# A list scheduler that fixes a kernel's instruction order: refitted costs, result time and hand-over apart, and a charge for changes of kind on TensorE

## The chip, the cores and the metric

The kernel runs on one core of one Trainium2 chip. A core has TensorE (PE, matrix products; its weight loads appear as PEld), VectorE (DVE), ScalarE (ACT), GpSimd (POOL) and SyncE (SP), each with an instruction queue of its own, and 16 DMA engines. The metric is the device time of one execution in microseconds, lower is better. Of several executions the median counts.

## The reference

Attention with a capped score over 4 batches of 12 heads (48 heads), 448 positions, head size 64, followed by a feed-forward layer with layer norm on the 1,792 tokens of 768 features, with 3,072 hidden features:

```
scores = scale * q @ k.T                      # per batch and head, 448 x 448
scores = cap * tanh(scores / cap)
attn = exp(scores - max); attn /= attn.sum(-1) + 1e-9
x = (attn @ v), heads side by side            # 1792 x 768
xn = (x - mean) / sqrt(var + 1e-6) * g_ln
out = x + relu(xn @ w_ch1) @ w_ch2            # all fp32
```

## The kernel before, in words

**Precision.** The feed-forward products have fp32 accuracy out of a narrower matmul type: every operand is split into a rounded part (hi) and a remainder (lo), and a product is three matmuls, hi*hi, hi*lo and lo*hi, that add up in one PSUM bank. Rounding and remainder of an operand are two instructions of ScalarE or VectorE (L488 and L495). The scores and the product with v run on plain fp32 operands; from head 28 on the scores too are split.

**Attention.** The 48 heads run in 12 groups of four. For each group TensorE makes blocks of scores (`qk`, L723 and, split, L749; "rest" blocks for the last 64 rows), ScalarE takes tanh (L768) and exp (L776) of them, TensorE multiplies by v (`pv`, L552 and L559), adds up the denominators (`sums`, L636, L640) and transposes for the division (`turn`, L662, L676). L609 copies a group's result out of its PSUM bank.

**Feed-forward, first six token tiles (of 128 tokens).** `up` (L1019 to L1021, six matmuls of 128x384 per operation) and `down` (L1048 to L1050) run between the attention groups, from the first norm (its transposes are L899) at about 76 us to about 500 us.

**Feed-forward, last eight token tiles.** In the last stage, from about 505 us, the product runs as a seven-product scheme of Strassen's kind, block by block over 12 blocks of hidden features. Per block there are two sorts of operation on TensorE:
- *W product n* (n = 1 to 7; `product` in `stage`, L1237, L1238, L1240): nine matmuls of 128x512 that make hidden features. Products 1, 6, 7 and 4 add up one after another in one PSUM bank (`pa`), 5 and 3 in a second, 2 has a third. After each of the four the copy `aside` (ScalarE, L1254) reads `pa`, and it must have done so before the next product adds to it. VectorE's `plus` (L1258) and `join` (L1274) combine the copies, `operand` splits the combination (L488, L495), and `hidden` (L1030, L1032) does ReLU and split.
- *T product k of tile m* (`product` in `thin`, L1330 to L1332): three matmuls of 128x384 that multiply a split operand by the second weight. A T product that starts a bank is evacuated by a copy (ScalarE, L1338) or a sum (VectorE, L1342) into one half of a staging buffer `st`; there are six of these. When both halves are in, GpSimd's `store` (L1347) adds the buffer to the output in DRAM by DMA, and the buffer is free once that has landed.

**What sets the order.** The program is written as a list of operations (`add`), each with an engine, a cost in ns, the buffers that it reads, writes and takes, and a due time worked out from the table `PLAN`. The class `Order` then plays the list through before the kernel is built: at each moment every free engine takes, of its ready operations, the one with the earliest due time whose buffers can be had. A consumer becomes ready at the producer's end plus `SAME` on the same engine (130 ns on VectorE, 155 on ScalarE, 0 on TensorE) or `CROSS` (210 ns) from another engine. A PSUM bank or staging buffer comes back when its last user's end, plus `CROSS`, has passed. `lag` is added to an operation's end: 170 ns for the W and T products (`PLAN["lag"]`), 2,500 ns for a store. The costs are straight lines in the operand's width n (`VEC1`, `VEC2`, `VECC` for VectorE, `ACTS`, `ACTP`, `ACTC` for ScalarE, `POOL1` for GpSimd, `MM` and `F4` for TensorE). The sequence in which this play takes the operations is then the program's order on each engine and each DMA queue. Nothing of the play runs on the chip: there each engine executes its fixed list and waits on semaphores.

The two lines that carry the timing of the play:

```python
free[e] = o.end = t + cost
c.ready = max(c.ready, o.end + (SAME[e] if e == c.engine and not o.dma else CROSS))
```

Of the kernel before, what the change touches and what calls it, by code (L numbers as in the profile page):

```python
# [15 lines left out]
ALU = mybir.AluOpType  # L16
PSUM = bass.MemoryType.PSUM

B, H, S, D = 4, 12, 448, 64
# [5 lines left out]
CC, FC = DM // 128, DFF // 128  # L25
NT = B * S // 128
HG = 4
HALF = DM // 2
# [12 lines left out]
TOK = 512  # L41
# [13 lines left out]
VEC1 = lambda n: 60 + 0.75 * n  # L55
VEC2 = lambda n: 50 + 1.1 * n
ACTS = lambda n: 20 + 0.99 * n
ACTP = lambda n: 20 + 1.0 * n
VECC = lambda n: 95 + 1.17 * n
ACTC = lambda n: 160 + 0.87 * n  # L60
POOL1 = lambda n: 100 + 1.1 * n
POOL2 = lambda n: 148 + 2.104 * n
MM = lambda n: n * 0.4515
F4 = lambda n: n * 1.76
TANH, EXP = 1000, 1260
SAME = {"V": 130, "A": 155, "G": 100, "T": 0, "S": 0}
CROSS = 210
# [28 lines left out]
    ks=3000, again=12000, down=16000, thin=20000, w3=14000, fetch=16000, near=20000, part=20000, w3b=0, both=32000, half=15000, u=2000, t=0, lag=170, landing=2500, chunk=18000, blocks=-42000,  # L96
# [47 lines left out]
class Op:  # L144
    __slots__ = ("engine", "cost", "fn", "due", "bufs", "left", "outs", "ready", "end", "dma", "seq", "wait", "after", "lag")


class Order:
# [9 lines left out]
    def add(self, engines, fn, reads=(), writes=(), allocs=(), due=0.0, dma=0, after=(), lag=0.0):  # L158
        op = Op()
        (op.engine, op.cost), = engines.items()  # L160
        op.fn, op.due, op.dma, op.lag, op.seq = fn, due, dma, lag, len(self.ops)
# [45 lines left out]
    def emit(self, realize, run):  # L207
# [8 lines left out]
        cold, busy, window = False, 0.0, -3000.0  # L216
# [21 lines left out]
        while pending:  # L238
            done = False
            for e in free:  # L240
# [15 lines left out]
                if e == "T":  # L256
# [3 lines left out]
                    cost *= 1 + cold  # L260
                    busy += cost
                free[e] = o.end = t + cost
# [16 lines left out]
                for c in o.outs:  # L279

                    if "P" not in (e, c.engine):
                        c.ready = max(c.ready, o.end + (SAME[e] if e == c.engine and not o.dma else CROSS))
# [97 lines left out]
class Program:  # L380
# [117 lines left out]
    def quad(self, i, at):  # L498
# [92 lines left out]
        else:  # L591
            for p in range(2):
                for blocks in [[j] for j in range(NK)] if i + p == 0 and not self.general else [range(NK)]:
                    add({"T": 200 + len(blocks) * F4(S)}, lambda e, p=p, blocks=blocks: pv(p, blocks),
                        reads=[*v_all, *(done(p) if len(blocks) > 1 else [(es[p], "e", j) for j in blocks])], writes=[pos[p]],
                        allocs=pos, due=dues[p] - PLAN["pv"] - rush)
            add({"T": 100 + F4(S)}, lambda e: pv_rest(), reads=[*v_all, er], writes=pos, due=dues[2] - PLAN["pv"] - rush)
# [31 lines left out]
    def sums(self, parts, rests, due, cost=0, first=None, reads=(), writes=()):  # L629
# [13 lines left out]
        self.last_pv = self.add({"T": 200 + (1 + len(rests)) * F4(S) + cost}, sums, reads=[*parts, *rests, *reads],  # L643
# [3 lines left out]
    def finish(self, i, pairs, ps, due, late):  # L647
# [16 lines left out]
        add({"T": 440}, turn, reads=[(ss, 0), (ss, 2)], writes=[pr], due=due)  # L664
# [6 lines left out]
        for j, tl, p in self.token_tiles(b):  # L671
# [6 lines left out]
            add({"T": len(pairs) * 110}, turn, reads=[(o, x) for o in pairs for x in (0, 2)] + [r] * self.general, writes=[pf], due=due)  # L678
# [899 lines left out]
```

## Time and profile before

| | before |
|---|---|
| device time, median of 3 runs | 857.84 us (857.4 to 928.27) |
| the profiled execution, its own time | 857.77 us |
| its span in the trace | 856.0 us |
| TensorE matmuls busy | 845.8 us (99%), 4700 instructions |
| VectorE busy | 701.7 us (82%) |
| ScalarE busy | 511.9 us (60%) |
| GpSimd busy | 152.1 us (18%) |
| DMA | 148.96 MB, mean 174 GB/s |

The span is the time from the first to the last recorded instruction; 1.8 us of the execution lie around it. Busy time of TensorE counts matmuls, whose ends are modelled; weight loads run beside them. A group of instructions is written as line, engine, operation, output<-inputs, shapes, count; then busy time and mean duration, and behind the bar the idle time of that engine just before these instructions, with what ended most of it. In a timeline a row holds start and duration in us and the same description, with `[idle before <- releaser]` at its end where there was idle time. `two` is a pair of PSUM banks, `y` a combination buffer of the last stage, `hop` a split operand, `w` a split weight, `X` a split combination of xn, `d` a pair of q and k rows, `b` an attention result, and `x` on the way to `out_dram` a staging buffer.

### The profile page before, as it was taken

The numbers are of one execution on the slowest core, as the hardware profiler recorded it, in microseconds if no ns is written. First come the engines' busy times: TensorE is split into PE (matmuls) and PEld (weight loads), VectorE is DVE, ScalarE is ACT, GpSimd is POOL, SyncE is SP. The second block draws the span as 40 slices with busy tenths as digits, with TensorE's granted clock in tenths as the row PEclk, the third lists the DMA queues.
The fourth block names the chain that finished last, engine by engine and source line by source line (L and its number), as shares of the span: only waits on it lengthen the run. The fifth ranks groups of instructions, "written<-read, shape, count | busy, mean of one in ns | idle before, by whom it ended". The sixth has DMA issues, their size and how long they took to land.

```text
span 856.0 us, 12856 instructions
## 1 busy us (share of the span) xinstructions
PE 845.8 (99%) x4700; PEld 706.4 (83%) x4700; DVE 701.7 (82%) x1157; ACT 511.9 (60%) x795; POOL 152.1 (18%) x198
## 2 busy tenths in 40 slices
PE   8999999999999999999999999999999999999997
PEld 5344477979879799799799989998988998999897
DVE  2689798878789878787689878888888888788896
ACT  6887877644654647354436646756575666566550
POOL 0134231111112111111110001223113212312210
PEclk9999999999999999999999999999999999999999
DMA  9597766665675774654562344798878888787984
GB/s 230 138 251 212 197 179 176 186 204 161 184 221 167 221 210 168 184 169 128 179 254 102 102 143 83 164 180 156 169 159 155 165 169 159 139 191 157 181 220 152
DMA packets 55579, 148.96 MB, mean 174 GB/s; under 512 B 7378, under 2 KB 20178, under 8 KB 55506
## 3 DMA queue, kind: packets, MB, share of 16 engines
q1 hardware_dynamic: 41328, 113.43, 44.8%
q0 software_dynamic: 12096, 33.04, 22.8%
q10 hardware_dynamic: 2082, 1.58, 0.6%
q8 instruction: 39, 0.64, 0.3%
q14 instruction: 34, 0.28, 0.1%
HBM read 87.46 MB, written 60.56 MB: 173 GB/s over the span
## 4 chain that ended last, share of the span: by engine, by line
PE 95%; ACT 2%; DVE 1%; issue 0%; POOL 0%; DVEq 0%; ACTq 0%
PE two L1237 7%; PE two L1330 7%; PE two L1240 7%; PE two L1332 7%; PE two L1331 7%; PE two L1238 7%; PE two L1019 6%; PE two L1048 6%; PE two L1050 6%; PE two L1049 6%; PE two L552 6%; PE two L1021 6%; PE two L1020 6%; PE two L723 6%; PE two L676 1%; PE two L636 1%
## 5 line engine op out<-in xcount | busy, mean ns | idle before, releaser
L1347 POOL DMA_DIRECT2D out_dram<-x x84 | 73.4, 998 | 314.6 <-ACT x L1338 227.2
L1338 ACT ACTIVATE x<-two 128x384 f32<-128x384 f32 x168 | 79.6, 487 | 35.6 <-PE two L1332 27.0
L1237 PE MATMUL two<-X,q 128*128 128x512 f32 x252 | 98.9, 392 | 1.2 <-ACT y L1254 1.2
L1019 PE MATMUL two<-hA,q 128*128 128x384 f32 x288 | 99.8, 347 | 0.0
L1240 PE MATMUL two<-X,q 128*128 128x512 f32 x252 | 98.8, 392 | 0.0
L1238 PE MATMUL two<-X,q 128*128 128x512 f32 x252 | 98.6, 391 | 0.0
L1342 DVE TENSOR_TENSOR x<-two,x 128x384 f32<-128x384 f32 x144 | 76.9, 552 | 26.3 <-PE two L1332 22.7
L1048 PE MATMUL two<-w,hh 128*128 128x384 f32 x288 | 98.3, 341 | 0.0
L1050 PE MATMUL two<-w,hl 128*128 128x384 f32 x288 | 97.2, 337 | 0.0
L1049 PE MATMUL two<-w,hh 128*128 128x384 f32 x288 | 97.1, 337 | 0.0
L1021 PE MATMUL two<-hA,q 128*128 128x384 f32 x288 | 96.9, 337 | 0.0
L1020 PE MATMUL two<-lA,q 128*128 128x384 f32 x288 | 96.8, 336 | 0.0
L951 POOL TENSOR_SCALAR raw<-raw 128x768 f32<-128x768 f32 x48 | 49.5, 1031 | 227.9 <-ACT c L947 213.6
L1330 PE MATMUL two<-w,hop 128*128 128x384 f32 x264 | 89.1, 338 | 0.0
L1332 PE MATMUL two<-w,hop 128*128 128x384 f32 x264 | 88.9, 337 | 0.0
L1331 PE MATMUL two<-w,hop 128*128 128x384 f32 x264 | 88.9, 337 | 0.0
L768 ACT ACTIVATE e<-two,sc 128x448 f32<-128x448 f32 (+1 forms) x108 | 75.0, 758 | 20.1 <-PE two L723 20.1
L1053 DVE TENSOR_TENSOR x<-two,x 128x384 f32<-128x384 f32 x144 | 76.2, 548 | 12.4 <-PE two L1050 12.1
L488 ACT ACTIVATE w<-c 128x768 fp32r<-128x768 f32 x38 | 32.1, 845 | 60.3 <-DVE c L956 22.9
L1019 PEld LDWEIGHTS two<-hA,q 128*128 128x128 f32 x288 | 54.1, 188 | 10.9 <-issue 7.1
L776 ACT ACTIVATE e<-e,capt 128x1344 f32<-128x1344 f32 (+1 forms) x35 | 61.1, 1770 | 0.3
L552 PE MATMUL two<-e,v 128*64 128x448 f32 x288 | 59.2, 547 | 1.1 <-ACT e L776 0.8
(179 smaller groups left out, 1852.1 us busy)
## 6 DMA issues: line engine op xcount, KB each, us to landing
raw<-in_w_dram SPq DMA_DIRECT2D x48, 768.0 KB, 5.0
out_dram<-x POOLq DMA_DIRECT2D x84, 384.0 KB, 7.2
kept<-c SPq DMA_DIRECT2D x47, 384.0 KB, 5.5
d<-in_kq_dram SPq DMA_DIRECT2D x48, 224.0 KB, 5.7
d<-kept SPq DMA_DIRECT2D x23, 384.0 KB, 3.2
c<-kept SPq DMA_DIRECT2D x23, 384.0 KB, 7.4
v<-in_v_dram SPq DMA_DIRECT2D x24, 227.5 KB, 5.8
x<-out_dram SPq DMA_DIRECT2D x13, 384.0 KB, 5.1
```

The costliest lines, as they stand in the source:

```text
L1019: nc.tensor.matmul(ps.ap[:, :n], lhsT=w1h.ap[:, wc], rhs=xh.ap[:, c], start=(c == 0), stop=False)
L1020: nc.tensor.matmul(ps.ap[:, :n], lhsT=w1h.ap[:, wc], rhs=xl.ap[:, c], start=False, stop=False)
L1021: nc.tensor.matmul(ps.ap[:, :n], lhsT=w1l.ap[:, wc], rhs=xh.ap[:, c], start=False, stop=(c == CC - 1))
L1048: nc.tensor.matmul(o, lhsT=h[0].ap[:, mc], rhs=w[0].ap[:, hc], start=(f == 0), stop=False)
L1049: nc.tensor.matmul(o, lhsT=h[0].ap[:, mc], rhs=w[1].ap[:, hc], start=False, stop=False)
L1050: nc.tensor.matmul(o, lhsT=h[1].ap[:, mc], rhs=w[0].ap[:, hc], start=False, stop=(f == last))
L1237: nc.tensor.matmul(ps.ap, lhsT=wh.ap[:, wc], rhs=xs[c].ap[:, 0], start=start and c == 0, **o)
L1238: nc.tensor.matmul(ps.ap, lhsT=wh.ap[:, wc], rhs=xs[c].ap[:, 1], start=False, **o)
L1240: nc.tensor.matmul(ps.ap, lhsT=wl.ap[:, wc], rhs=xs[c].ap[:, 0], start=False, **o)
L1330: nc.tensor.matmul(o, lhsT=hh.ap[:, mc], rhs=wh.ap, start=begin, stop=False, **skip)
L1331: nc.tensor.matmul(o, lhsT=hh.ap[:, mc], rhs=wl.ap, start=False, stop=False, **skip)
L1332: nc.tensor.matmul(o, lhsT=hl.ap[:, mc], rhs=wh.ap, start=False, stop=True, **skip)
```

## The change

Five things, all in the numbers by which `Order` plays the list through:

1. The cost lines are other straight lines: `VEC1`, `VEC2`, `ACTS`, `ACTP`, `ACTC`, `POOL1`, `F4`, the tanh and exp, and several single costs; `VECC` goes, and its users take `VEC2`. At a width of 512 a VectorE operation that reads PSUM or two operands was charged 694 ns and is now charged 595; at 384 it was 544 and is 459.
2. A producer's result comes `TAIL` after its engine is free again: 83 ns on VectorE, 110 on ScalarE, 70 on GpSimd, 163 on TensorE. The engine itself goes on to its next operation without the tail.
3. The hand-over to any consumer is `CROSS`, 35 ns instead of 210, on top of the tail; `SAME` goes. From one TensorE operation to the next there is neither.
4. Every TensorE operation has a `kind`. When the kind differs from that of the operation before, `SHIFT` of the kind that is left is charged. Constants of 100 and 200 ns that stood in the costs of single operations go.
5. `PLAN["lag"]` is 0 instead of 170, the GpSimd power of the norm costs 1,600 instead of 800, and the store on GpSimd 860 instead of 1,200.

The core of the diff:

```diff
-VEC1 = lambda n: 60 + 0.75 * n
-VEC2 = lambda n: 50 + 1.1 * n
-ACTS = lambda n: 20 + 0.99 * n
-ACTP = lambda n: 20 + 1.0 * n
-VECC = lambda n: 95 + 1.17 * n
-ACTC = lambda n: 160 + 0.87 * n
-POOL1 = lambda n: 100 + 1.1 * n
+VEC1 = lambda n: 45 + 0.63 * n
+VEC2 = lambda n: 50 + 1.065 * n
+ACTS = lambda n: 92 + 0.835 * n
+ACTP = lambda n: 130 + 0.66 * n
+ACTC = lambda n: 11 + 0.94 * n
+POOL1 = lambda n: 100 + 1.04 * n
-F4 = lambda n: n * 1.76
-TANH, EXP = 1000, 1260
-SAME = {"V": 130, "A": 155, "G": 100, "T": 0, "S": 0}
-CROSS = 210
+F4 = lambda n: n * 1.6786
+TANH, EXP = 888, {1: 1305, 2: 2441}
+TAIL = {"V": 83, "A": 110, "G": 70, "T": 163, "S": 0, "P": 0}
+CROSS = 35
+SHIFT = dict(up=98, down=50, fp=200, split=190, pv=150, rest=160, sums=137, turn=-80)
...
-                    cost *= 1 + cold
+                    cost = cost * (1 + cold) + (SHIFT.get(kind, 0) if o.kind != kind else 0)
+                    kind = o.kind
                     busy += cost
-                free[e] = o.end = t + cost
+                free[e] = t + cost
+                o.end = free[e] + TAIL[e]
...
-                        c.ready = max(c.ready, o.end + (SAME[e] if e == c.engine and not o.dma else CROSS))
+                        c.ready = max(c.ready, o.end + CROSS - (TAIL[e] + CROSS) * (e == c.engine == "T"))
...
-                    add({"T": 200 + len(blocks) * F4(S)}, lambda e, p=p, blocks=blocks: pv(p, blocks),
+                    add({"T": len(blocks) * F4(S)}, lambda e, p=p, blocks=blocks: pv(p, blocks), kind="pv",
...
-            add({"V": VECC(TOK)}, lambda e: nc.vector.tensor_tensor(out=y.ap, in0=ps.ap, in1=y.ap, op=ALU.add),
+            add({"V": VEC2(TOK)}, lambda e: nc.vector.tensor_tensor(out=y.ap, in0=ps.ap, in1=y.ap, op=ALU.add),
```

No instruction is added or removed on any engine; each source line has as many instructions on each engine as it had. What moves is the order. Three places on TensorE follow. Lines of the changed kernel are 2 higher; the numbers in the names are those of the two builds and tell buffers apart within one build.

First, the fourth group of heads, where the trace of before stands at 53 to 60 us. `L723` is a score block, `L662` the transposes of a finished group, `L559` the rest of the product with v, `L636` and `L640` the denominators' sums. Before:

```order
L723 MATMUL two_228<-d_282 128x448 x2
L662 MATMUL two_227<-ident,b_235 128x128 x4
L559 MATMUL two_227<-d_77,v_242 64x448
L559 MATMUL two_226<-d_77,v_229 64x448
L559 MATMUL two_227<-d_77,v_242 64x448
L559 MATMUL two_226<-d_77,v_229 64x448
L723 MATMUL two_225<-d_291 128x448 x2
L723 MATMUL two_228<-d_291 128x448 x2
L723 MATMUL two_227<-d_291 128x448 x2
```

After:

```order
L725 MATMUL two_225<-d_284 128x448 x2
L638 MATMUL two_226<-d_254,ones 32x448 x2
L638 MATMUL two_226<-d_299,ones 32x448 x2
L642 MATMUL two_226<-d_77,ones 32x448 x4
L561 MATMUL two_228<-d_77,v_242 64x448
L561 MATMUL two_226<-d_77,v_229 64x448
L561 MATMUL two_228<-d_77,v_242 64x448
L561 MATMUL two_226<-d_77,v_229 64x448
L725 MATMUL two_227<-d_290 128x448 x2
L725 MATMUL two_225<-d_290 128x448 x2
L725 MATMUL two_228<-d_290 128x448 x2
```

The sums have moved ahead of the rest products, into the place where the transposes stood; the transposes come behind the score blocks.

Second, the step from W product 6 to W product 7, on TensorE, in a block that stands at about 589 us in the trace of before. `L1237` to `L1240` are the last three matmuls of product 6 and the first three of product 7, `L1330` to `L1332` a T product. Before:

```order
L1237 MATMUL two_226<-X_4095,q_67 128x512
L1238 MATMUL two_226<-X_4095,q_67 128x512
L1240 MATMUL two_226<-X_4095,q_70 128x512
L1330 MATMUL two_228<-w_72,hop_4404 128x384
L1331 MATMUL two_228<-w_72,hop_4404 128x384
L1332 MATMUL two_228<-w_72,hop_4404 128x384
L1237 MATMUL two_226<-X_3825,q_4216 128x512
L1238 MATMUL two_226<-X_3825,q_4216 128x512
L1240 MATMUL two_226<-X_3825,q_68 128x512
```

After, in a block of the new steady pattern (the last three rows are the first of W product 2; W product 7 follows when its nine are through):

```order
L1239 MATMUL two_228<-X_4099,q_67 128x512
L1240 MATMUL two_228<-X_4099,q_67 128x512
L1242 MATMUL two_228<-X_4099,q_4208 128x512
L1332 MATMUL two_226<-w_73,hop_4375 128x384
L1333 MATMUL two_226<-w_73,hop_4375 128x384
L1334 MATMUL two_226<-w_73,hop_4375 128x384
L1332 MATMUL two_227<-w_72,hop_4432 128x384
L1333 MATMUL two_227<-w_72,hop_4432 128x384
L1334 MATMUL two_227<-w_72,hop_4432 128x384
L1239 MATMUL two_226<-X_3747,q_4186 128x512
L1240 MATMUL two_226<-X_3747,q_4186 128x512
L1242 MATMUL two_226<-X_3747,q_69 128x512
```

Between products 6 and 7 there stood one T product; now two T products and W product 2 stand there.

Third, T product 4 of tile 2, on TensorE, in a block in the middle of the last stage. Before it stood behind W product 7, and T product 3 of the tile (the last three rows) followed:

```order
L1237 MATMUL two_228<-X_4048,q_4231 128x512
L1238 MATMUL two_228<-X_4048,q_4231 128x512
L1240 MATMUL two_228<-X_4048,q_67 128x512
L1330 MATMUL two_227<-w_71,hop_4415 128x384
L1331 MATMUL two_227<-w_71,hop_4415 128x384
L1332 MATMUL two_227<-w_71,hop_4415 128x384
L1330 MATMUL two_226<-w_71,hop_4415 128x384
L1331 MATMUL two_226<-w_71,hop_4415 128x384
L1332 MATMUL two_226<-w_71,hop_4415 128x384
```

After, it stands behind W product 5, which itself follows 24 T products without a W product between; T product 3 of the tile follows, then the first rows of W product 6:

```order
L1239 MATMUL two_226<-X_4068,q_69 128x512
L1240 MATMUL two_226<-X_4068,q_69 128x512
L1242 MATMUL two_226<-X_4068,q_4186 128x512
L1332 MATMUL two_227<-w_73,hop_4342 128x384
L1333 MATMUL two_227<-w_73,hop_4342 128x384
L1334 MATMUL two_227<-w_73,hop_4342 128x384
L1332 MATMUL two_227<-w_72,hop_4432 128x384
L1333 MATMUL two_227<-w_72,hop_4432 128x384
L1334 MATMUL two_227<-w_72,hop_4432 128x384
L1239 MATMUL two_225<-X_3823,q_69 128x512
L1240 MATMUL two_225<-X_3823,q_69 128x512
L1242 MATMUL two_225<-X_3823,q_4186 128x512
```

From there on a block reads, in the new order: W5, two T products, W6, two T products, W2, W7, W1 of the next block, W4, W3, and 24 T products. Before, W and T products alternated in shorter runs: behind the first W product, TensorE goes from one kind to another 126 times before and 70 times after.

## Rows read from the trace of the kernel before

**Rows 1.** Busy time by stretch (us, busy of each engine, granted clock, DMA).
```profile
core 0: us, PE busy (x) PEld busy (x) DVE busy (x) ACT busy (x) POOL busy (x), PEclk, DMA share, GB/s
...
20.00:80.00 60.00, 59.04 (x357) 23.17 (x353) 47.51 (x78) 53.89 (x50) 18.53 (x25) 1.00 0.75 202
80.00:440.00 360.00, 360.00 (x2169) 297.88 (x2168) 296.64 (x466) 203.50 (x288) 58.70 (x74) 1.00 0.62 185
...
520.00:800.00 280.00, 279.50 (x1411) 254.17 (x1410) 236.87 (x403) 175.31 (x334) 66.70 (x77) 1.00 0.82 161
800.00:856.00 56.00, 50.38 (x260) 46.17 (x259) 46.70 (x81) 21.36 (x38) 6.67 (x8) 0.98 0.72 186
sum 856.00, PE 845.84 PEld 706.37 DVE 701.66 ACT 511.90 POOL 152.08; mean PE 140.97 PEld 117.73 DVE 116.94 ACT 85.32 POOL 25.35
```

**Rows 2.** Waits of TensorE: who waited <- for whom: sum in us, count, longest.
```profile
PE two L1237 <- ACT y L1254: 1.2, 4, 0.7
```

**Rows 3.** Timeline from 51 to 59 us: start, us, what, [idle before <- releaser].
```profile
51.51 0.96 PE L636 MATMUL two<-d,ones 128*32 128x448 f32 x8
...
53.15 1.02 PE L723 MATMUL two<-d 64*128 64x448 f32 x4
...
54.10 0.66 PE L662 MATMUL two<-ident,b 128*128 128x128 f32 x4
54.22 1.01 ACT L768 ACTIVATE e<-two,sc 128x896 f32<-128x896 f32 x1 [0.39 <-PE two L723]
...
54.69 0.98 PE L559 MATMUL two<-d,v 64*64 64x448 f32 x8
...
55.26 2.54 ACT L776 ACTIVATE e<-e,capt 128x2688 f32<-128x2688 f32 x1
55.60 2.52 PE L723 MATMUL two<-d 64*128 64x448 f32 x10
...
57.70 0.96 ACT L609 ACTIVATE b<-two 128x448 f32<-128x448 f32 x2
...
58.29 1.02 PE L723 MATMUL two<-d 64*128 64x448 f32 x2 [0.16 <-ACT b L609]
```

**Rows 4.** Timeline from 589 to 591 us, W product 6 to W product 7.
```profile
589.27 0.39 PE L1240 MATMUL two<-X,q 128*128 128x512 f32 x1
...
589.50 0.34 PE L1330 MATMUL two<-w,hop 128*128 128x384 f32 x1
...
589.70 0.60 ACT L1254 ACTIVATE y<-two 128x512 f32<-128x512 f32 x1 [1.22 <-PE two L1240]
...
589.85 0.33 PE L1332 MATMUL two<-w,hop 128*128 128x384 f32 x1
...
590.35 0.50 PE L1237 MATMUL two<-X,q 128*128 128x512 f32 x1 [0.17 <-ACT y L1254]
```

**Rows 5.** Groups of instructions by line, the rounding and the join of the last stage.
```profile
L488 ACT ACTIVATE hop<-y 128x512 fp32r<-128x512 f32 x39 | 24.6, 630 | 5.7 <-DVE y L1274 5.5
...
L1274 DVE SCALAR_TENSOR_TENSOR y<-y,y 128x512 f32<-128x512 f32 x34 | 23.2, 683 | 0.4 <-ACT y L1254 0.4
```

**Rows 6.** Timeline from 612 to 623 us, staging buffers and their store.
```profile
612.59 0.96 ACT L1338 ACTIVATE x<-two 128x384 f32<-128x384 f32 x2 [1.18 <-PE two L1332]
...
613.38 1.75 POOL L1347 DMA_DIRECT2D out_dram<-x  x2 [14.17 <-ACT x L1338]
...
620.93 0.49 ACT L1338 ACTIVATE x<-two 128x384 f32<-128x384 f32 x1 [0.64 <-DMA out_dram<-x]
...
622.24 0.34 PE L1330 MATMUL two<-w,hop 128*128 128x384 f32 x1
```

**Rows 7.** All 84 stores of L1347, from issue to landing.
```profile
DMA to landing us min/median/max: 4.5/7.2/12.7
```

**Rows 8.** Timeline from 70 to 77 us, weight steps and the first norm.
```profile
71.08 0.95 DVE L495 TENSOR_TENSOR w<-c,w 128x768 fp32r<-128x768 f32 x1
...
71.95 0.95 DVE L956 SCALAR_TENSOR_TENSOR c<-c,raw 128x768 int32<-128x768 int32 x1
...
76.12 1.07 PE L899 MATMUL two<-ident,xn 128*128 128x128 f32 x6 [0.79 <-DVE lA L908]
```

## What the change should do to the time, predicted before it ran

> **What bounds the kernel now.** I read the busy times by stretch first, then TensorE's own waits, and last the timeline at those waits. The reader should see one engine that is full. TensorE is busy for 845.84 of 856.00 us, at a granted clock of 1.00 in every stretch shown but the last, where the work ends; from 80 to 440 us it is busy for all of the 360 us [rows 1]. What it does not use is small and in known places: 1.0 us between 20 and 80 us (60.00 less 59.04), 0.5 us between 520 and 800 us, 5.6 us in the last stretch (56.00 less 50.38), which is mostly the evacuation and the store behind the last product, and the rest at start-up and in the stretch left out [rows 1]. Waits that the trace names for it: four before L1237, 1.2 us together [rows 2], one on L609 [rows 3] and one on L908 [rows 8]. A matmul's end is modelled, so a stall can also hide inside a busy run; I therefore measure stalls from start to start in the timeline. VectorE comes next with 236.87 us busy of 280 in the main stretch of the last stage, ScalarE with 175.31 [rows 1].
>
> So a new order can win some microseconds at most, and can lose whatever it makes TensorE wait.
>
> **What the change removes, adds and moves.** It removes and adds no instruction: I counted the rows of the two orders, and each engine has the same number of instructions from each source line in both (4,308 matmuls on TensorE). Only their order moves. Hence the sum is made of waits alone, against the profiled execution: 856.0 us of span and 1.8 us around it, 857.77 us, beside a median of 857.84.
>
> *Changes of kind.* The planner now charges TensorE for going from one kind of product to another. The orders differ little where that costs anything: up to the first W product TensorE changes kind 175 times before and 177 times after. Behind it, the runs fall from 126 to 70. A W-to-T border is free in the trace: the first T matmul starts 0.23 us after the last W matmul (589.27 to 589.50), which is the W matmul's own interval [rows 4]. Sum for this part: 0.
>
> *The early stall, gained.* In the fourth group of heads TensorE stands before its last score block. The run that starts at 55.60 us needs 1.70 us for its first two blocks (0.95 for the first, as 53.15 to 54.10 shows, and 0.75 for the second, which pays no change of kind), yet the third starts at 58.29, so 1.0 us is lost. The bank it wants is freed by the copy L609 at 57.70, which stands on ScalarE behind tanh at 54.22 and the exponential at 55.26 [rows 3]. From the end of the block that feeds the tanh to the third block's start are 4.19 us (54.10 to 58.29). Before, four transposes, the rest products and two score blocks lie between, 54.10 to 57.30, 3.2 us. In the new order the sums lie there in place of the transposes (1.64 us, 51.51 to 53.15): with the rest products (0.91, 54.69 to 55.60) and the two blocks that makes 4.25 us against 4.19 wanted [rows 3]. I take the whole 1.0 us as gained; if the copy is late by more than 0.06 us, that much comes back.
>
> *Three stalls of the last stage, gained.* W product 7 adds to the bank of W product 6, so the copy L1254 must have read it first. In three of the twelve blocks only one T product stands between: TensorE is through with it at 590.02 (589.85 and one interval of 0.17) and starts at 590.35, 0.33 us later, because the copy starts at 589.70 and takes 0.60 us [rows 4]. In the new order two T products and W product 2 stand there in every block but the first and the last, 0.53 + 0.53 + 2.05 = 3.1 us (three intervals of 0.175 and nine of 0.228); the wait from W to W is 0.85 us (589.50 to 590.35) [rows 4]. Gain 3 x 0.33 = 1.0 us. The fourth such wait, 0.7 us in the first block, is the longest [rows 2]; it stays, since product 7 follows 6 directly in both orders.
>
> *New tight places, lost.* With `lag` at 0 the 24 T products behind W product 3 now run without a break. Three covers shrink. (a) T product 4 of a tile follows T product 7 of it by two T products, 1.06 us, where in most blocks it was three or more; result and copy between need 0.20 + 0.49 us [rows 4, 6]. Slack 0.3 us, if nothing stands before the copy on ScalarE. (b) T product 5 follows W product 4 by W product 3 and three T products, 2.05 + 1.58 = 3.6 us, where it was 6.2. The chain of result 0.20, copy 0.60, join 0.68, rounding 0.63, remainder about 0.68 and three handovers is about 2.9 us [rows 4, 5]. Slack 0.7 us. (c) The store. Six staging buffers serve eight halves per block, so the copy of T product 7 of tile 2 waits until the store of tile 0, filled by T product 4, has landed, and T product 4 of tile 2 waits for that copy. Cover from the end of T4 of tile 0 to the start of T4 of tile 2: eleven T products and one W product, 7.9 us, where it was 9.9 to 10.9. Chain: copy 0.5, issue 0.3 later, landing, copy 0.5, handovers 0.2, so landing plus 1.5. In the trace the pair at 612.59 is issued from 613.38, and the copy that waits for the second landing runs at 620.93, while its product starts at 622.24 or later [rows 6]. All such stores land in 4.5 to 12.7 us, median 7.2 [rows 7]; the one for tile 0 is issued first, and the copy behind it shows no wait in that block while the one behind the second does, so I put it near 6: 7.5 us of chain against 7.9 of cover. For all three I take 0.2 us in all.
>
> The Trainium skill has a rule for the landing (DMA: Bandwidth & Descriptors, Anatomy of one DMA): about 2.0 us and bytes over 436e3, an estimate of 2.9 us for 384 KB. By it the chain would be 4.4 us and (c) no risk at all. The trace disagrees: not one of the 84 stores landed under 4.5 us [rows 7], so the risk stays in my range.
>
> *The norm, unchanged.* The transposes L899 at 76.12 waited 0.8 us for VectorE [rows 8]. Now four more transposes stand before them (0.6 us of cover, 54.10 to 54.69 [rows 3]), but a weight step of 0.87 us stands before the VectorE work they wait for (71.08 to 71.95 is such a step) [rows 8]. Between -0.8 and +0.3 us; I take 0. The order of loads on SyncE's queue and of stores on GpSimd's moves with the rest; TensorE waited for no load, and the first 38 entries of SyncE's queue are the same loads in the same order.
>
> Sum: 857.8 - 1.0 - 1.0 + 0.2 = **856.0 us**.
>
> **The rivals.** *No gain left over.* The waits go elsewhere in the crowded start, where ScalarE is busy 53.89 of 60 us [rows 1]: each stall removed there hands ScalarE the next one. For it: the early stall's cover is exceeded by only 0.06 us. Against: later covers there are longer. Then 1.3 us or more come back: 857.3 to 859.
>
> *Slower: the store's landing becomes TensorE's wait.* Place: T4 of tile 2, in some ten blocks. Each microsecond of landing over 6.4 us costs 10 us. At the median of 7.2 us that is 0.8 x 10 = 8 us, 864. It decides for slower by 2% (17.2 us) at a landing of 8.1 us, 875. For it: half of all stores take 7.2 us or more [rows 7]. Against: the slow ones should be those queued behind others, and this one is first.
>
> *VectorE cannot go at engine time.* The planner now charges it 595 ns for a 512-wide operation and lets the result come 83 ns later; it charged 694 before. If VectorE took the next only with the result out, the some 13 operations queued around chain (b) would be 1.1 us late, 0.4 us more than the slack, times ten blocks: 860. Against: a step of 0.95 us started at 71.08 and the next at 71.95, 0.08 us before its end [rows 8]. A rule in the Trainium skill speaks for this rival (VectorE: DVE Perf Modes, The DRAIN you can't avoid): the next operation does not start until the pipe is empty. By that rule the time would be about 860; the trace disagrees, with 0.87 us from start to start against 0.95 us of duration.
>
> *Faster by more than 2%* would need 17.2 us out of 10.2 us of idle time; it takes shorter matmuls, and nothing here changes them.
>
> **How the numbers follow.** The forecast's own case, 852.5 to 857.3, gets 0.62; at its lower end every stall goes that can (1.0 and 0.8 early, 1.0 and 0.7 in the last stage) and 1.8 us more that hide in busy runs. No gain left, 857.3 to 859: 0.23. The landing: 0.10, of which 0.06 up to 864 and 0.04 past 875. VectorE at result time, 860: 0.04. Over 2% faster: 0.01. The range of 852.5 to 862 leaves out the landing's upper part, the last case and some of what lies at the cases' own edges, under 2 in 10 together. With 2% as about what a measurement here can tell from no change: faster 0.01, within 2% 0.94, slower 0.05.
>
> **What would show it right or wrong.** In the profile after (lines there are 2 higher): TensorE within 2 us of 845.8 busy; no wait of a score block on the copy L611 near 58 us; one wait before L1239 on L1256 in place of four, of about 0.7 us; no wait of TensorE over 0.1 us per block at L1332. A wait there once per block, behind a copy L1340 that waits for a store, is the landing rival; one at T product 5, behind the remainder L497, is VectorE's. The forecast is wrong if the first 120 us lose more than they did, or if TensorE's intervals within a kind move.

## The result, and the profile after

The changed kernel takes 862.66 us (median of 6 runs) against 858.03 us for the kernel before, measured beside it: a ratio of 1.0057, interval 1.0045 to 1.0069, that is 4.9 us (3.9 to 5.9) slower. One execution of each kernel took far longer than the others (928.27 and 1,681.19 us), and the ratio leaves it out. Forecast were 856.0 us within 852.5 to 862.0, so the time lies above the range and on the other side of no change.

The stretches of the profile after, in the columns of [rows 1], with its lines:

```profile
core 0 of [0], span 860.8 us
...
20.00:80.00 60.00, 57.61 (x360) 22.98 (x357) 48.55 (x84) 53.63 (x51) 19.95 (x29) 1.00 0.79 209
80.00:440.00 360.00, 359.33 (x2148) 295.58 (x2147) 291.78 (x461) 203.30 (x285) 60.10 (x70) 1.00 0.62 183
520.00:800.00 280.00, 278.95 (x1406) 252.63 (x1407) 232.45 (x402) 172.73 (x334) 68.18 (x78) 1.00 0.80 159
800.00:860.00 60.00, 53.32 (x274) 48.67 (x272) 46.91 (x81) 23.11 (x40) 5.41 (x7) 0.98 0.65 174
```

TensorE is busy for less in each of the first three: 57.61 of 60 us where it had 59.04, 359.33 where it had all 360, 278.95 where it had 279.50 [rows 1]. The waits that the trace names for it (who waited <- for whom: us together, times, longest):

```profile
PE two L901 <- DVE lA L910: 1.1, 1, 1.1
PE two L1239 <- ACT y L1256: 0.9, 1, 0.9
PE two L1332 <- ACT x L1340: 0.8, 2, 0.6
PE two L1334 <- DVE hop L497: 0.6, 1, 0.6
PE two L1023 <- DVE q L497: 0.5, 1, 0.5
PE two L725 <- DVE x L688: 0.5, 1, 0.5
PE two L751 <- ACT e L770: 0.5, 1, 0.5
PE two L901 <- DVE x L1055: 0.4, 1, 0.4
PE two L678 <- ACT e L770: 0.2, 1, 0.2
```

Four waits between W product 6 and 7 [rows 2] have become one, of 0.9 us, as forecast. All the others in this list but the first, which was 0.79 us long [rows 8], are new: single waits at places that had none.

**Where the time went, in one table.** Waits that last less than a matmul do not show as idle time, so I laid TensorE's work along both traces. Each matmul counts as the mean interval to the next one of its line and shape (from the traces of before and after, 84 to 840 us, with pauses cut off); the sum of these is its work done, and the time of the next start less that work is how far it is behind. The columns are the growth of that between five marks of work; it is negative where matmuls follow closer than their mean interval. In the trace of before these marks stand at 68, 141, 501, 542 and 842 us, so the inner columns are the crowded start's second half, the middle, the first block of the last stage and the steady blocks. The early stall at 58 us [rows 3] lies ahead of the first mark. Then come the time from the last matmul's start to the end of the span, and the span. The rows e_... are the experiments below.

```
                behind at 50 | 50-115  115-480  480-520  520-820 | to the end  span
before               18.0    |   7.9    -5.1      0.8      0.3   |    5.9     856.0
before, again        17.7    |   8.0    -5.3      0.8      0.3   |    7.3     856.9
after                16.5    |   9.9    -4.2      3.0     -0.4   |    7.9     860.8
after, again         17.2    |   9.9    -3.8      3.4      0.1   |    8.4     863.4
e_start              18.1    |   9.9    -5.5      0.8      0.3   |    8.2     860.0
e_last_old           16.9    |  10.0    -3.7      0.8      0.3   |    7.8     860.1
e_last_new           17.2    |   7.9    -5.3      2.2     -0.3   |    5.7     855.4
e_lag                16.7    |   9.9    -3.7      3.5     -1.5   |    6.3     859.2
e_land               17.4    |   9.9    -3.7      2.3      2.1   |    6.8     862.8
e_second_lag         17.8    |   8.0    -5.1      0.8      1.2   |    5.6     856.3
e_smooth             17.3    |   9.3    -5.3      0.9     -0.1   |    6.8     856.9
```

The four inner columns depend on the order: rows with the same order there agree to 0.5 us, with two exceptions. The 9.3 of e_smooth has the order of before, and a wait of 0.9 us of a sum for VectorE which no other execution has. In the first block e_last_new reads 2.2 and not 3.0 to 3.5: TensorE's order is the same there, but the wait behind a store (below) does not occur in it. By the two rows of either kernel the change costs 2.0 us in the second half of the crowded start, 0.9 to 1.5 in the middle and 2.2 to 2.6 in the first block, and gives 0.2 to 0.7 in the steady blocks: about 5 us, the 4.9 that were measured. The first column and the time to the end say little of the order: two executions of one program differ by 0.7 us in the one and 1.4 in the other. Where exactly the marks' columns divide the loss also depends, by some tenths, on where a pause is cut off.

Some points need no such mean, since by then both kernels have executed the same matmuls by line and shape. The rows give the start of the next one, in us (behind 2,972 it is the first W product 7):

```
matmuls done               160    284    316    344    412    606    722    854   1118   2972
before                   34.36  54.10  60.26  65.64  77.55 109.75 129.70 149.88 193.37 507.05
after                    33.05  52.94  59.04  64.06  75.96 108.78 129.79 150.39 195.02 508.68
after less before        -1.31  -1.16  -1.22  -1.58  -1.59  -0.97  +0.09  +0.51  +1.65  +1.63
after, again, less before -0.63 -0.48  -0.53  -0.89  -0.89  -0.28  +0.80  +1.21  +2.32  +2.72
```

Up to 1,118 matmuls the two executions of the changed kernel show the same steps. Over the place of the early stall, from 284 to 316 matmuls, the change gains 0.06 us, and 0.4 us up to 344. From 412 to 854, which is 78 to 150 us before, it loses 2.1 us, and 1.1 more up to 193 us.

**The crowded start.** Timeline of TensorE and ScalarE after, where [rows 3] is the one before:

```profile
52.46 2.54 ACT L778 ACTIVATE e<-e,capt 128x2688 f32<-128x2688 f32 x1
53.85 2.64 PE L725 MATMUL two<-d 64*128 64x448 f32 x12
54.90 1.39 ACT L611 ACTIVATE b<-two 128x448 f32<-128x448 f32 x3
56.17 2.81 ACT L770 ACTIVATE e<-two,sc 128x896 f32<-128x896 f32 x3
57.24 0.66 PE L678 MATMUL two<-ident,b 128*128 128x128 f32 x4
58.14 0.44 PE L678 MATMUL two<-ident,b 128*128 128x128 f32 x2 [0.24 <-ACT e L770]
59.04 0.98 PE L751 MATMUL two<-d 64*64 64x448 f32 x8 [0.46 <-ACT e L770]
```

The twelve matmuls of the three score blocks run without a break (2.64 us): the wait on the copy is gone, as forecast. But ScalarE is full there from 52.46 on, now with three copies between the exponential and the tanh, so the tanh comes at 56.17, and the transposes and the rest block behind, whose banks it must read, wait 0.24 and 0.46 us. What was gained at the blocks is lost behind them: 6.16 us from 284 to 316 matmuls before, 6.10 after.

Further on, two waits stand where the kernel before has none:

```profile
79.62 1.35 PE L725 MATMUL two<-d 64*128 64x448 f32 x4 [0.50 <-DVE x L688]
...
123.56 0.55 PE L901 MATMUL two<-ident,xn 128*128 128x128 f32 x3 [0.45 <-DVE x L1055]
```

**The last stage.** First block: T product 5 (519.09 to 520.21) waits in its middle for the remainder that VectorE makes, and T product 4 of tile 2 (536.32) for a copy that itself stood until a store had landed. `PEld` and queue rows are left out.

```profile
519.27 0.34 PE L1333 MATMUL two<-w,hop 128*128 128x384 f32 x1
520.21 0.45 PE L1334 MATMUL two<-w,hop 128*128 128x384 f32 x1 [0.61 <-DVE hop L497]
520.50 0.34 PE L1332 MATMUL two<-w,hop 128*128 128x384 f32 x1
...
527.61 3.76 POOL L1349 DMA_DIRECT2D out_dram<-x  x4 [90.69 <-DVE x L1344]
...
535.44 0.33 PE L1334 MATMUL two<-w,hop 128*128 128x384 f32 x1
...
535.78 0.49 ACT L1340 ACTIVATE x<-two 128x384 f32<-128x384 f32 x1 [2.57 <-DMA out_dram<-x]
...
536.32 0.44 PE L1332 MATMUL two<-w,hop 128*128 128x384 f32 x1 [0.55 <-ACT x L1340]
536.60 0.34 PE L1333 MATMUL two<-w,hop 128*128 128x384 f32 x1
```

A steady block has one short wait instead, which the list of waits does not name:

```profile
553.66 1.65 ACT L1340 ACTIVATE x<-two 128x384 f32<-128x384 f32 x4
...
553.91 0.68 DVE L497 TENSOR_TENSOR hop<-y,hop 128x512 fp32r<-128x512 f32 x1
...
554.35 0.34 PE L1334 MATMUL two<-w,hop 128*128 128x384 f32 x1
...
554.60 0.44 PE L1332 MATMUL two<-w,hop 128*128 128x384 f32 x1
554.88 0.34 PE L1333 MATMUL two<-w,hop 128*128 128x384 f32 x1
```

T product 4 of tile 0 starts 0.25 us after the matmul ahead of it instead of 0.174, when the second of four queued copies is through (553.66, some 0.4 later, and 0.49 long), and the matmul behind it 0.28 us later instead of 0.174. The wait of 0.08 us costs 0.18, in nine blocks 1.65 us.

### The profile page after: what moved, and what is told of

Read it like the earlier page. It is cut to its first block, busy times and chain, and to the rows that moved or that the text cites. A ratio compares the mean times of both kernels' runs of the same rounds, so it can differ in the third digit from the quotient of the medians.

```text
span 860.8 us, 12865 instructions
## 1 busy us (share of the span) xinstructions
PE 844.2 (98%) x4700; PEld 702.1 (82%) x4700; DVE 695.8 (81%) x1157; ACT 510.2 (59%) x795; POOL 155.1 (18%) x198
## 4 chain that ended last, share of the span: by engine, by line
PE 77%; issue 12%; DVE 6%; ACT 2%; DMA 1%; POOL 1%; DVEq 0%; POOLq 0%; ACTq 0%
PE two L1332 7%; PE two L1334 6%; PE two L1333 6%; PE two L1239 6%; PE two L1242 6%; PE two L1240 6%; PE two L1021 5%; PE two L725 5%; PE two L554 4%; PE two L1023 4%; PE two L1022 4%; PE two L1050 4%; PE two L1051 4%; PE two L1052 4%; DVE c L958 1%
## 5 line engine op out<-in xcount | busy, mean ns | idle before, releaser
L1344 DVE TENSOR_TENSOR x<-two,x 128x384 f32<-128x384 f32 x140 | 72.3, 551 | 50.0 <-PE two L1334 46.7
L1240 PE MATMUL two<-X,q 128*128 128x512 f32 x252 | 98.2, 390 | 0.0
L953 POOL TENSOR_SCALAR raw<-raw 128x768 f32<-128x768 f32 x48 | 53.5, 1119 | 222.1 <-ACT c L949 221.6
L1340 ACT ACTIVATE x<-two 128x384 f32<-128x384 f32 x168 | 73.2, 493 | 33.8 <-PE two L1334 22.6
L1332 PE MATMUL two<-w,hop 128*128 128x384 f32 x264 | 90.1, 341 | 0.8 <-ACT x L1340 0.8
L1055 DVE TENSOR_TENSOR x<-two,x 128x384 f32<-128x384 f32 x144 | 76.1, 548 | 11.1 <-PE two L1052 10.8
L490 ACT ACTIVATE w<-c 128x768 fp32r<-128x768 f32 x28 | 23.7, 845 | 82.8 <-PE two L1052 31.8
```

What stands on the lines that cost most here:

```text
L1240: nc.tensor.matmul(ps.ap, lhsT=wh.ap[:, wc], rhs=xs[c].ap[:, 1], start=False, **o)
L1332: nc.tensor.matmul(o, lhsT=hh.ap[:, mc], rhs=wh.ap, start=begin, stop=False, **skip)
```

## The experiments

In the hybrids the planner keeps both sets of numbers and takes one or the other by its own clock, in which the first W product stands at 484.1 us in the changed kernel and at 492.0 in the kernel before (in the traces it starts at 493.16 and 491.38). They share one edit; only the four conditions differ:

```diff
+COSTS = lambda t: t >= 485000
+KINDS_CHARGED = lambda t: t >= 485000
+HANDOVER = lambda t: t >= 485000
+LAG = lambda t: t >= 485000
...
-                cost = o.cost
+                cost, handover, charged = o.cost, HANDOVER(t), KINDS_CHARGED(t)
+                if isinstance(cost, Two):
+                    cost = (cost.new if COSTS(t) else cost.old) + (cost.fresh if charged else cost.flat)
...
-                o.end = free[e] + TAIL[e]
+                o.end = free[e] + TAIL[e] * handover
...
-                o.end += o.lag
+                o.end += (0 if LAG(t) else 170) if e == "T" and o.kind is None else o.lag
```

With all four true the order is that of the changed kernel, with all four false that of the kernel before. Ratios are to the kernel before on the same chip (858.26, 858.30 and 858.37 us in the three groups).

**By stage.** e_last_new has the conditions above; e_last_old has `t < 478000` in all four.

> The planner works with its old numbers up to shortly before the last stage and with all the new ones from there on; the last stage's order on TensorE is then that of the changed kernel, everything ahead of it that of the kernel before. Theory A (the loss is made of single stalls where the trace of the changed kernel shows them, and the stages add): the last stage brings stalls of 0.8, 0.45 and 0.7 us in its first block and takes three of 0.33 us away, about +1.1 us, so 859.1 us; if the 1.9 us at the program's end (from the last matmul to the end 7.5 us instead of 5.6) belong to this order too, 861. Theory B (the new order ahead of the last stage leaves it in a worse state, and the last stage's own order is a gain): 857.0, below the kernel before.

Measured: 859.17 us, 1.0015 (1.0006 to 1.0025), so 1.3 us (0.5 to 2.1) slower, where theory A had 859.1 and theory B a gain. One of theory A's three stalls, the 0.7 us behind a store, is not in this trace: the store in question landed 6.44 us after its issue here, and 7.33, 7.62 and 7.82 us in after, e_again and e_lag, which all have the wait.

> The other way round: new numbers up to shortly before the last stage, old ones from there on. Theory A: the stalls ahead of the last stage alone, net +1.5 us by the position of TensorE at 485 us of work in the two traces, so 859.5 us, with the three waits of 0.33 us between W product 6 and 7 back and the end of the program as before (5.6 us behind the last matmul). Theory B: nearly the whole loss, 861 to 862.5 us, since the last stage starts in the worse state.

Measured: 861.78 us, 1.0036 (1.0024 to 1.0049), 3.1 us (2.1 to 4.2) slower. The time is the one that theory B gives, but its reason is out: the last stage's new order is a loss by itself (e_last_new), and behind the new early part the last stage with its old order reads 0.8 and 0.3 us in the table, as in the kernel before. The two parts add up within their intervals, 1.3 + 3.1 = 4.4 of 4.9 us; the wait behind the store, 0.8 us with the late matmul after it, is in neither. Theory A's own number for the early part, 1.5 us, was too low, since it took in the first 50 us, where the changed kernel's execution was 1.5 us ahead by something that no order explains (below).

**The start alone**, `t < 125000` in all four conditions:

> All the new numbers for the crowded start alone (up to 125 us of the plan), the old ones from there on. Theory A (the early loss is made in the start, 2.1 us between 50 and 140 us of TensorE's work, and the middle adds 1.2 of its own): 860.4 us, TensorE's lag behind its own work 2.1 us more at 140 than at 50 us of it and as in the kernel before from there. Rival (the start's order is harmless, its loss is regained in the middle, where TensorE has spare feed-forward work): 858.3 us.

Measured: 859.47 us, 1.0012 (1.0003 to 1.0021), 1.0 us (0.3 to 1.8) slower. The table shows the same 9.9 us between 50 and 115, 2.0 more than before, and some 0.3 of it regained behind. So the start is a loss of its own and is hardly regained; its size is between the two expectations. The rest of the early loss, 3.1 less 1.0, is the middle's; the table has 0.9 to 1.5 there.

**Which of the numbers.** Each part alone up to 478 us, the old numbers from there on: costs (`COSTS = lambda t: t < 478000`, the others `False`), hand-over, kinds.

> Only the refitted costs, and only up to shortly before the last stage; hand-over, kinds and the last stage are as before. The whole early part of the change cost 3.1 us measured (3.3 by TensorE's position: 2.1 between 50 and 140 us of its work, 1.2 from there to 480). Theory A (shorter VectorE and ScalarE costs bring transposes and score blocks forward onto results that are not there yet): 861 us, most of the 3.1. Rival (no part does it alone; any renumbering upsets the crowded start by 0 to 2 us): 858.5 to 860 us for each of the three parts.

> Only the new result and hand-over times (35 ns and the tail of the engine instead of 130 to 210 ns), up to shortly before the last stage. Theory A (the costs do it): 858.3 us, as before. Rival (no part alone): 858.5 to 860 us. Theory C (the hand-over is now planned too short): 861 us.

> Only the charge for changes of kind in place of the constants, up to shortly before the last stage. Theory A (the costs do it): 858.3 us. Rival (no part alone): 858.5 to 860 us. Theory D (the charge splits the second norm's transposes and moves them ahead of their operands): 861 us, with waits of TensorE for VectorE at the transposes near 123 us.

Measured: costs 873.07 us, 1.0162 (1.0141 to 1.0183); hand-over 863.06 us, 1.0052 (1.0036 to 1.0068); kinds 860.23 us, 1.0026 (1.0016 to 1.0037). So 13.9, 4.5 and 2.2 us where all three together cost 3.1. The first is not all early: with the costs alone the order of the last stage is not that of the kernel before either, and by TensorE's position some 9 us are lost ahead of it and some 4.5 in it. In the other two the last stage has the order of before. Theories A, C and D each name one guilty part, and since each part costs something by itself none of them holds as the whole cause. Of D's run the number and the sign came true (861 lies inside its interval, and the transposes at 123.06 us wait 1.16 us for `lA`); the changed kernel has 0.45 us at that place, for another operand. The rival had the direction (each part costs something), but the size only for the kinds, whose interval reaches below 860. The costs alone are the worst: TensorE's score blocks and the norm's transposes wait for VectorE's `lA` (its line is 937 there), and a `down` for `x`, so the order has them ahead of what is ready:

```profile
PE two L752 <- DVE lA L937: 2.4, 1, 2.4
PE two L928 <- DVE lA L937: 2.3, 3, 1.7
PE two L752 <- ACT d L797: 1.7, 1, 1.7
PE two L1077 <- DVE x L1082: 1.3, 1, 1.3
```

**The last stage's covers.** e_lag is the changed kernel with `LAG` false throughout, e_land with `landing=5000`.

> The changed kernel with the lag of W and T products back at 170 ns in the planner. The order ahead of the last stage and in its first block does not differ by that; from the second block on T product 4 of tile 2 stands behind W product 6 instead of between 5 and 6. Theory A (the stalls come from the first block and the early part): 862.7 us, as the changed kernel, within 0.5. Rival (the missing slack behind W and T products makes the stalls): the waits of 0.6 to 0.9 us in the last stage go, 860.7 us.

Measured: 861.04 us, 1.0034 (1.0020 to 1.0048). The time is nearer to the rival's 860.7, but its waits do not go: the first block's stay (3.5 us in the table), as theory A has it, and it is the steady blocks that gain 1.1 to 1.6 us more. The reason is not in the expectation: with the lag a third T product stands between T products 7 and 4 of tile 0, and the short wait of 0.18 us per block is gone.

> The changed kernel with the landing of a store planned at 5000 ns beyond its transfer instead of 2500, so that W product 2 stands ahead of T product 4 of tile 2 in the blocks. Theory A: the wait of 0.7 us of T product 4 of tile 2 behind a copy that waits for a store goes, the one of 0.45 us perhaps too: 861.5 to 862.0 us. Rival (the landing matters nowhere, the waits are ScalarE's queue): 862.7 us, and the wait of 0.7 us stays.

Measured: 863.98 us, 1.0064 (1.0050 to 1.0079), which neither has. In the first block the wait behind the store is gone (2.3 us in the table where the changed kernel's two traces have 3.0 and 3.4; but e_last_new is without it too, with the old landing time), and the steady blocks lose 2.1: the pattern changes from block to block, and a T product waits behind a store again, 0.76 us:

```profile
674.78 0.87 ACT L1367 ACTIVATE x<-two 128x384 f32<-128x384 f32 x2 [1.22 <-DMA out_dram<-x]
...
675.32 0.44 PE L1359 MATMUL two<-w,hop 128*128 128x384 f32 x1 [0.76 <-ACT x L1367]
```

**Versions meant to be faster.** e_second_lag takes costs, hand-over and kinds from 540 us of the plan on and leaves `LAG` false; e_smooth takes them from 544 us on, with `LAG = lambda t: t < 585000`.

> The planner works with its old numbers through the early part and the first block of the last stage, and from the second block on with the new costs, hand-over and kinds, but with a lag of 170 ns. Theory A (the losses sit in the crowded early part and in the last stage's first block, the steady blocks are a gain of 1.8 us where the lag keeps T product 4 of tile 2 behind W product 6): 1.8 us under the kernel before, 856.4 us, the waits of 0.33 us between W product 6 and 7 gone and no wait of 0.6 us or more but that of the first block's product 7. Theory B (the last stage's gain is the spread of single executions): 858.3 us.

Measured: 859.79 us, 1.0017 (1.0007 to 1.0028), 1.5 us slower, above both theories.

> The early part as before; in the last stage old numbers with a lag of 0 through its first block, then the new ones, and the lag of 170 ns again from the fourth block on, so that no W product 7 or 4 follows directly on the one whose copy it needs, and the steady blocks read W5, W6, four T products, W2, W7, W1, W4, W3 and 24 T products. Theory A: first block and change-over as before, 0.15 us less in each of the eight steady blocks and the two later waits of 0.43 us gone: 1.3 to 1.8 us under the kernel before, 856.5 to 857.0 us. Theory B (the steady blocks are no gain): 858.3 us or more.

Measured: 859.46 us, 1.0013 (1.0002 to 1.0024). Neither beats the kernel before. For e_smooth that is theory B's number, but not its reason, since the steady blocks do gain: in e_smooth TensorE is 23.6 us behind at 580 us of work and 22.1 at 800, where before it stays at 22.0. The change-over between the patterns takes that back. In e_second_lag W product 4 follows W product 7 directly, twice, and waits for its copy (ScalarE's line is 1283 there):

```profile
568.33 0.49 PE L1266 MATMUL two<-X,q 128*128 128x512 f32 x1 [0.69 <-ACT y L1283]
...
599.04 0.51 PE L1266 MATMUL two<-X,q 128*128 128x512 f32 x1 [1.25 <-ACT y L1283]
```

In e_smooth one T product waits 0.7 us behind a store's landing in the change-over. That leaves about nothing by the trace, and the measured 1.1 us (0.2 to 2.1) does not contradict that by much.

**Both kernels once more.**

> The changed kernel once more, for what differs from one execution to the next. Theory A (the first 7 us and the time from the last matmul to the end are no part of the order): TensorE's waits between are the same to 0.1 us, and the first tanh (6.96 us in the first trace) and the 7.5 us at the end are each off by 0.5 us or more. Rival (both belong to the program): the same within 0.2 us, 862.6 us.

> The kernel before once more, for the same: its first tanh came at 8.28 us and its end 5.6 us behind the last matmul. Theory A: one or both are off by 0.5 us or more, the waits between the same. Rival: the same within 0.2 us, 857.8 us.

Measured: 865.17 and 858.67 us, one execution each. The changed kernel, the first tanh and the last matmul's row, of the first trace and of the second:

```profile
core 0 of [0], span 860.8 us
...
6.96 1.01 ACT L770 ACTIVATE e<-two,sc 128x896 f32<-128x896 f32 x1 [1.42 <-PE two L725]
...
852.99 0.34 PE L1334 MATMUL two<-q,X 128*128 128x384 f32 x1
```

```profile
core 0 of [0], span 863.4 us
...
7.64 1.01 ACT L770 ACTIVATE e<-two,sc 128x896 f32<-128x896 f32 x1 [2.31 <-PE two L725]
...
854.94 0.34 PE L1334 MATMUL two<-q,X 128*128 128x384 f32 x1
```

The kernel before, likewise:

```profile
core 0 of [0], span 856.0 us
...
8.28 1.01 ACT L768 ACTIVATE e<-two,sc 128x896 f32<-128x896 f32 x1 [2.93 <-PE two L723]
...
850.04 0.34 PE L1332 MATMUL two<-q,X 128*128 128x384 f32 x1
```

```profile
core 0 of [0], span 856.9 us
...
7.97 1.01 ACT L768 ACTIVATE e<-two,sc 128x896 f32<-128x896 f32 x1 [2.75 <-PE two L723]
...
849.56 0.34 PE L1332 MATMUL two<-q,X 128*128 128x384 f32 x1
```

The changed kernel's first tanh is off by 0.7 us, its end by 0.5 (7.9 and 8.4 us behind the last matmul's start). Of the kernel before the first tanh is off by 0.3, the end by 1.4 (5.9 and 7.3). Its waits between are the same; the changed kernel's are but for the one behind the store, 0.6 and 0.7 us. So theory A: first and last microseconds belong to the execution. That the changed kernel's two ends are long says nothing of its order either, since e_last_new, with the same order in the last stage, has 5.7 us.

## Why the prediction was wrong, point by point

- **One full engine, only waits count: right.** TensorE's busy time moved by 1.6 us (845.8 to 844.2), its idle time by much more.
- **Three stalls between W product 6 and 7, gained: right, a little small.** They are gone. Each was worth 0.43 us, not 0.33: behind the late start the next matmul also came 0.11 us late.
- **The early stall, gained: the step that failed first.** The stall itself went, but of the 1.0 us that the sum takes as gained 0.06 came by the end of that stretch (6.16 us before, 6.10 after, for the same 32 matmuls) and 0.4 by 66 us. The rest moved some 2.5 us on, to the transposes and the rest block. The rival "no gain left over" had this mechanism, ScalarE handing on the next stall, but it reached to 859 us only, with a chance of 0.23. I worked out the cover at one place and did not follow ScalarE's queue to what stood next in it.
- **The rest of the start: at nothing in the sum.** It loses 2.1 us between 78 and 150 us, where I had looked at the first norm's transposes alone. What the trace names there is 0.50 us at a score block (79.62) and 0.45 at the second norm's transposes (123.56), both behind VectorE, each with 0.11 more for the next matmul; most of the remaining 0.9 us hides in busy runs.
- **The middle: not in the sum either.** It costs 0.9 to 1.5 us by the table. Between 189.6 and 193.4 us, where transposes stand, 0.8 us are lost, 0.13 of them shown as a wait, and behind a weight's remainder at 483 us 0.5 us.
- **New tight places, 0.2 us in all: mis-sized.** (a) was given 0.3 us of slack "if nothing stands before the copy on ScalarE". A copy stood before it, and it costs 0.18 us in nine blocks, 1.65 us. (b) and (c) hold in the steady blocks, which have no wait there. But I took the steady block for all of them. The first block has another order and issues four stores in a row, and there both break: 0.77 us at T product 5 (519.27 to 520.21, less 0.174), 0.45 at the T product 4 behind it, 0.71 at T product 4 of tile 2 (535.44 to 536.32, less 0.174), each with 0.11 more for the next matmul, and the wait of W product 7 grew from 0.85 to 1.02. The 0.71 us are the rival of the landing, once instead of in ten blocks, and not in every execution of that order (e_last_new). The first block is 2.2 to 2.6 us slower than before; why VectorE's chain is late there was not tried.
- **The landing.** The store behind that last wait was the second of the four at 527.61 (0.9 us apart, so issued near 528.5), and its copy started at 535.78: about 7.3 us, close to the median of [rows 7]. I had put the landing near 6 us, with 6.4 as the bound; one of 6.44 in e_last_new made no wait. The Trainium skill's rule (DMA: Bandwidth & Descriptors, Anatomy of one DMA), about 2.0 us and the bytes over the rate, gives an estimate of 2.9 us and no wait there; the trace disagrees again.
- **VectorE at result time: out.** If VectorE took the next operation only with the result out, T product 5 would be late in every block; it waits in the first alone, and in the block shown a remainder of 0.68 us starts at 553.91, 0.47 us after an operation of 0.55 us began at 553.44. The Trainium skill (VectorE: DVE Perf Modes, The DRAIN you can't avoid) has the next operation wait until the pipe is empty, but it says in the same place that one that is not held starts earlier, and the trace agrees with the latter:

```profile
553.44 0.55 DVE L497 TENSOR_TENSOR q<-d,q 128x384 fp32r<-128x384 f32 x1
```

- **Changes of kind at nothing: right for their borders.** From 545 us of work to 820 the interval from a W to a T product is 226 ns in the median (226 before), from T to W 176.5 (174 before).
- **The norm, taken at 0 between -0.8 and +0.3:** its first wait is 1.1 us where it was 0.8, the upper edge.

So the forecast's gain was there only in part, and what took its place were waits of 0.2 to 0.9 us scattered over the crowded start, the middle and the first block. They come from no one number of the change: by TensorE's position each of its parts alone upsets the start as much as the three together or more. What stays open is why this planner, whose single costs come nearer to the traced durations, makes the worse order. One thing can be read from its own clock: the old plan has the first W product 0.7 us later than the trace, the new one 9.0 us earlier. So the costs together came no nearer to the chip, and a plan that runs ahead counts on operands that are not there yet. That this makes the waits is argued and not shown; the runs show that the three parts depend on each other, not which rule would mend it.

## What to carry to other kernels

Where one engine is 99% busy, a new order can win only the few waits that the trace names, and it can lose a little anywhere; a loss of 0.6% was some twenty short waits, most of them far under 1 us. So look at the stretches where other engines are full too (the start) and at the blocks that are not yet steady (the first), not only at the steady block, and follow the queue of the engine that releases, not only the place where a stall goes away. Single costs that come nearer to the trace do not make the plan come nearer: lay the plan's clock beside the trace as a whole. And before a difference of a microsecond is read from two traces, look how far two executions of one program lie apart.

## What the runs showed that was not expected

- A wait of TensorE costs more than its length: after each late start the next matmul starts 0.28 us later instead of 0.174 (536.32 to 536.60, 554.60 to 554.88), so a wait of 0.08 us cost 0.18.
- The 24 first score matmuls have the same order in both kernels, and the first tanh behind them came at 8.28, 7.97, 6.96 and 7.64 us. The granted clock reads 1.00 in both, with fewer matmuls in the same microsecond before than after; what makes them slower in one execution stays open.

```profile
6.00:7.00 1.00, 1.00 (x4) 0.69 (x4) 0.00 (x0) 0.00 (x0) 0.00 (x0) 1.00 1.02 226
```

```profile
6.00:7.00 1.00, 1.00 (x7) 0.52 (x8) 0.00 (x0) 0.04 (x1) 0.00 (x0) 1.00 0.96 201
```

- With the new steady pattern the mean interval between matmuls of W products is 228.2 ns instead of 229.3 (pauses over 260 ns left out), in both traces of the changed kernel; over some 560 of them that is 0.6 us, about as much as the steady blocks gain on balance. Between T products there is no such difference: 174.7 ns in one trace of the changed kernel and 175.3 in the other, as before (175.3). What shortens the former was not tried.
